# Attention of a fused three-layer kernel in units of four heads, its scores on all four tiles of TensorE's array

## The chip, the core and the metric

The kernel runs on one core of one Trainium2 chip. The metric is device time in microseconds, the median of several executions. The engines of the core are named as the profile names them: PE (TensorE, matrix products; PEld is its weight load), ACT (ScalarE), DVE (VectorE), POOL (GpSimd) and SP (SyncE, which issues the DMAs). PE writes to PSUM alone, eight banks of 2 KB per partition; ACT and DVE read it from there.

## What is computed

Three layers follow each other. The first is attention inside chunks of 64 tokens (8 sequences, 8 heads, 576 tokens, 64 features a head); the second a gated layer with a convolution over three tokens; the third a token and feature transform (real part of a two-dimensional FFT), a normalization and two products.

```python
q, k, v = (x.reshape(8, 8, 9, 64, 64) for x in (q, k, v))   # 9 chunks of 64 tokens
s = matmul(q, k.T) / 8
a = exp(s - max(s)); a = a / (sum(a) + 1e-9)
x = matmul(a, v)                                            # -> (8, 576, 512)
h = relu(x @ w_in)
x = (h * sigmoid(conv3(h, conv_w))) @ w_out
u = x + real(fft2(x))
un = (u - mean(u)) / sqrt(var(u) + 1e-6)
out = u + relu(un @ w_ch1) @ w_ch2
```

## The kernel before

A planner orders the work. Every piece is an `op` with an engine, an estimated cost, a priority and the buffers that it reads and writes; `Plan.emit` goes through them by earliest start and then by priority, and calls the function that issues the instructions. The order on each engine is thus fixed when the program is built; what a buffer's ring allows is part of it (a ring of n buffers lets the op for a new one start when the readers of the n-th before are through). PSUM has two rings of four banks: `x`, used in turn, and `o`, whose banks are taken in any order. For `o` an op may ask for `spare` banks beside those that it takes: it starts only when as many are free, which keeps banks for others.

**Attention** (`attention(i, hp, prio)`, L339) handles half a sequence `i` (four blocks of 64 tokens when `i` is even, five when it is odd; `n` is that number) and one pair of heads `hp`. q and k lie transposed with the features of the first head on partitions 0 to 63 and those of the second on 64 to 127. `qk_unit` (L350) makes the scores, one 64x64x64 fp32 matmul for each block and head; the rows of a head's features set the row half of the array, the output's partitions the column half, and both are the same half here. All go to one PSUM bank `s`. DVE takes the maximum (L360), ACT the exponential of each block with its row sum (L365), DVE normalizes (L368 to L370). `tr_unit` (L374) transposes two blocks at a time, ACT copies them out (L381, L383), and `pv_unit` (L389) multiplies with v. There the token block's parity sets the row half and the head the column half, and the outputs of the two row halves go to two banks (L385). ACT copies them (L400, L403), and from the second half sequence on DVE makes the low part of a high/low split (L404). PE sees an fp32 matmul as two records; a split fp32r product is one record each for high by high, high by low and low by high.

**The gated layer** is `m_step` (L409) and `x_step` (L472), eight feature tiles `f` for each half sequence, one after the other on PE; `m_step` accumulates in an `o` bank, `x_step` in four `x` banks. Attention of half sequence `i + 1` is queued among the steps of `i` (L919). In the first half sequence the weights are also brought from their 64-bit form to fp32 on DVE (`to_float32`, L263).

**The transforms** follow each whole sequence `b`: `fold` (L522), six `d_step`s (L541) over features and three `s_step`s (L568) over tokens, two `o` banks each, then `u_step` (L598), which transposes, adds and stores `u`.

**The last layer** multiplies by Strassen-like block sums with seven products. `prep` (L765) loads, normalizes and transposes a chunk `c` of tokens and makes sums of its four blocks; `left` (L687) splits each into high and low part. `group(c, g, t)` (L795) computes the seven products of one of eight weight groups; its `product` may carry an `after`: for the very first group, `last_d`, the last `d_step`. `second` (L844) multiplies with the second weights. The weight sums of groups 2 to 7 live in a pool `e` that takes the place of the transforms' pools, so their casts (`load_tw`, L673) come after the transforms' last store.

The lines of `pv_unit` that set its tiles, and the call that gates the first group:

```python
for h2, k in [(h2, k + par) for k in range(0, n, 2) for h2 in range(2) for par in range(min(2, n - k))]:
    j, par = divmod(k, 2)
    kk = slice(64 * par, 64 * par + 64)
    mm = slice(64 * h2, 64 * h2 + 64)
    pe.matmul(xp[par]()[mm, j, :], v()[kk, j, mm], at()[kk, j, mm], start=True, stop=True)
...
return op("PE", mm_cost(n, passes=6), unit, prio, r=[*w, *x], w=[acc], after=() if c or g else last_d)
```

Of the kernel before, what the change touches and what calls it, by code (L numbers as in the profile page):

```python
# [8 lines left out]
F32 = mybir.dt.float32  # L9
# [37 lines left out]
class Buf:  # L47
# [16 lines left out]
    def __call__(self):  # L64
# [4 lines left out]
        return self.tile  # L69

# [129 lines left out]
def kernel(  # L200
# [88 lines left out]
    def load_dft(prio):  # L289
# [18 lines left out]
        h = buf("d", "fg", 1, [128, 640], F32R)  # L308
# [10 lines left out]
    early += [("d", tag, 1) for tag in ("f00", "f10", "f01", "f11", "fg")]  # L319
# [16 lines left out]

    x0 = {}

    def attention(i, hp, prio):  # L339
        b, c = divmod(i, 2)  # L340
        n = NTOK[c] // 64
        m = 2 + c
        qk = buf(*(("s", "xlo", 2) if (i, hp) == (0, HP - 1) else ("a", "qk", 3)), [128, 2, NTOK[c]])
        load(qk, lambda: (qk_a, qk_b)[c][b, hp], 1024 * NTOK[c], prio - 12)
        v = buf("a", "v", 6, [128, m, 128])
        load(v, lambda: (v_a, v_b)[c][b, hp], 65536 * m, prio - 10)
# [12 lines left out]
        es, mx, sm = buf("a", "es", 4, [128, n, 64]), buf("a", "mx", 4, [128, n]), buf("a", "sm", 4, [128, n, 1])  # L359
        vop(64 * n, lambda: dve.tensor_reduce(out=mx(), in_=s(), op=ALU.max, axis=AX.X), prio, [s], [mx])  # L360
        vop(n, lambda: dve.tensor_scalar(mx(), mx(), -0.125, None, op0=ALU.mult), prio, [mx], [mx])

        def exp():
            for k in range(n):
                act.activation(out=es()[:, k, :], in_=s()[:, k, :], func=ACT.Exp, scale=0.125, bias=mx()[:, k:k + 1], accum_out=sm()[:, k, :])  # L365

        op("ACT", 291 * n, exp, prio, r=[s, mx], w=[es, sm])
        vop(n, lambda: dve.tensor_scalar(sm(), sm(), 1e-9, None, op0=ALU.add), prio, [sm], [sm])  # L368
# [5 lines left out]
        def tr_unit():  # L374
            flat = es().rearrange("p c k -> p (c k)")
            for j in range(m):
                w = 64 if j == 2 else 128
                pe.transpose(tp()[:w, j, :], flat[:, 128 * j:128 * j + w], ident)  # L378
# [712 lines left out]
```

## Time and profile before

| | |
|---|---|
| median of three runs | 1398.34 us (1395.86 to 1398.58) |
| the profiled execution, its own time | 1399.52 us |
| its span, first to last instruction | 1397.7 us |
| PE busy | 1364.1 us (98%) |
| DVE busy | 1058.5 us (76%) |
| ACT busy | 818.5 us (59%) |
| bytes moved by DMA | 207.86 MB |
| granted clock of TensorE, mean | 0.995 |

The span has four stretches. Up to about 56 us the first half sequence and the weight conversions; to 634 us the other half sequences with attention, gated layer and transforms; to 1037 us the end of the transforms and the first products of the last layer (L815); to the end its second products (L882). A busy time is the union of an engine's instructions; PE's records overlap, so the time that a burst takes from PE is read from the starts of the records around it. A wait in square brackets behind a row is idle time of that engine just before it, with what ended it.

### The profile page before, as it was taken

The page shows a single profiled execution, that of the slowest core. Times are in us where ns is not written, and L with a number is a line of the kernel's source. Part 1 is how long each engine was busy: PE and PEld are TensorE (multiplying, and loading weights), DVE is VectorE, ACT ScalarE, POOL GpSimd, SP SyncE. Part 2 cuts the span into 40 slices and gives each one's busy share as a digit, 9 for nine tenths or more (in the row PEclk, how much of TensorE's full clock was granted, in tenths as well). Part 3 has the DMA queues.
Part 4 walks back from the last instruction along what each step waited for, and adds up shares of the span by engine and source line. Part 5 has one row for each costly group of instructions (what it writes and reads, how often), then busy time and mean ns, then how long its engine had stood idle before and what let it go on. Part 6 is the DMA issues. An engine that isn't in the chain of part 4 may idle for free.

```text
span 1397.7 us, 30248 instructions
## 1 busy us (share of the span) xinstructions
PE 1364.1 (98%) x11488; PEld 1323.3 (95%) x11488; DVE 1058.5 (76%) x2174; ACT 818.5 (59%) x2278; POOL 60.8 (4%) x182
## 2 busy tenths in 40 slices
PE   6899999999999999998999999999999999999999
PEld 5799999999999999998899999999999999999998
DVE  7999887878977676767576767576589777777773
ACT  6878575767776676755675655655664333333331
POOL 0101010101101000100000000000000000000000
PEclk9999999999999999999999999999999999999999
DMA  8534424323432222115756656666965545544541
GB/s 304 165 96 128 144 82 135 112 96 112 143 105 67 67 68 87 43 57 204 224 178 203 188 178 184 184 206 221 300 201 187 169 137 162 166 156 141 170 139 38
DMA packets 154721, 207.86 MB, mean 149 GB/s; under 512 B 11600, under 2 KB 103376, under 8 KB 154576
## 3 DMA queue, kind: packets, MB, share of 16 engines
q1 hardware_dynamic: 154576, 205.93, 46.2%
q8 instruction: 91, 1.49, 0.4%
q14 instruction: 54, 0.44, 0.1%
HBM read 131.82 MB, written 74.06 MB: 147 GB/s over the span
## 4 chain that ended last, share of the span: by engine, by line
PE 89%; DVE 4%; ACT 3%; DMA 2%; issue 1%; POOL 0%; ACTq 0%; SPq 0%; DVEq 0%; POOLq 0%
PE x L815 20%; PE x L882 15%; PE x L492 14%; PE o L427 13%; PE o L882 11%; PE o L557 3%; PE o L586 3%; PE o L815 3%; PE o L356 2%; PE o L394 2%; PE o L606 1%; PE o L717 1%; PE o L378 1%; DVE raw L729 1%; DMA ts<-t_scr 1%; ACT es L365 1%
## 5 line engine op out<-in xcount | busy, mean ns | idle before, releaser
L255 ACT CAST sxh<-raw 128x1024 fp32r<-128x1024 f32 (+1 forms) x145 | 142.4, 994 | 190.1 <-PE o L882 81.9
L427 PE MATMUL o<-x,wih 128*128 128x320 f32 (+1 forms) x960 | 201.0, 302 | 1.7 <-ACT at L383 0.9
L815 PE MATMUL x<-sxh,th 128*128 128x384 f32 x576 | 195.2, 339 | 4.6 <-ACT th L255 2.1
L815 PE MATMUL x<-sxl,th 128*128 128x384 f32 x576 | 193.6, 336 | 1.6 <-DVE sxl L256 1.6
L815 PE MATMUL x<-sxh,tl 128*128 128x384 f32 x576 | 193.5, 336 | 0.3 <-DVE tl L256 0.3
L256 DVE TENSOR_TENSOR sxl<-raw,sxh 128x1024 fp32r<-128x1024 f32 (+1 forms) x145 | 165.6, 1153 | 30.2 <-ACT sxh L255 30.0
L882 PE MATMUL x<-th,sxl 128*128 128x256 f32 x576 | 163.1, 283 | 0.5 <-DVE sxl L256 0.5
L882 PE MATMUL x<-th,sxh 128*128 128x256 f32 x576 | 163.1, 283 | 0.0
L882 PE MATMUL x<-tl,sxh 128*128 128x256 f32 x576 | 163.0, 283 | 0.0
L791 DVE TENSOR_TENSOR u<-x,u 128x384 f32<-128x384 f32 (+1 forms) x168 | 83.6, 499 | 104.6 <-PE x L815 34.6
L427 PEld LDWEIGHTS o<-x,wih 128*128 128x128 f32 x960 | 152.8, 188 | 4.7 <-ACT at L383 1.2
L444 DVE SCALAR_TENSOR_TENSOR cv<-h,cw,cv 128x255 f32<-128x255 f32 (+2 forms) x256 | 130.8, 514 | 34.2 <-ACT cv L458 20.3
L492 PE MATMUL x<-gh,woh 128*128 128x322 f32 (+1 forms) x480 | 148.1, 309 | 0.1
L492 PE MATMUL x<-gl,woh 128*128 128x322 f32 (+1 forms) x480 | 142.3, 296 | 0.1
L492 PE MATMUL x<-gh,wol 128*128 128x322 f32 (+1 forms) x480 | 142.1, 296 | 0.0
L427 PE MATMUL o<-x,wil 128*128 128x320 f32 (+1 forms) x480 | 142.0, 296 | 0.0
L882 PE MATMUL o<-th,sxl 128*128 128x256 f32 x432 | 122.3, 283 | 0.0
L882 PE MATMUL o<-tl,sxh 128*128 128x256 f32 x432 | 122.2, 283 | 0.0
L882 PE MATMUL o<-th,sxh 128*128 128x256 f32 x432 | 122.2, 283 | 0.0
L815 PEld LDWEIGHTS x<-sxh,th 128*128 128x128 f32 x576 | 108.8, 189 | 7.0 <-ACT u L799 3.0
L815 PEld LDWEIGHTS x<-sxl,th 128*128 128x128 f32 x576 | 108.9, 189 | 2.4 <-DVE sxl L256 2.4
L882 PEld LDWEIGHTS x<-th,sxl 128*128 128x128 f32 x576 | 110.6, 192 | 0.7 <-DVE sxl L256 0.7
(266 smaller groups left out, 3301.5 us busy)
## 6 DMA issues: line engine op xcount, KB each, us to landing
raw<-h_scr SPq DMA_DIRECT2D x72, 512.0 KB, 4.4
h_scr<-u SPq DMA_DIRECT2D x96, 192.0 KB, 3.1
u<-u_scr SPq DMA_DIRECT2D x66, 256.0 KB, 4.6
qk<-in_qk_b SPq DMA_DIRECT2D x32, 320.0 KB, 3.0
h_scr<-m SPq DMA_DIRECT2D x48, 192.0 KB, 2.7
h_scr<-h SPq DMA_DIRECT2D x48, 192.0 KB, 2.9
out_y<-u SPq DMA_DIRECT2D x35, 256.0 KB, 2.4
wide<-in_w_ch SPq DMA_DIRECT2D x16, 512.0 KB, 5.1
```

The lines of the kernel that those rows point to most:

```text
L255: aop(n, lambda: act.copy(out=cut(h()), in_=cut(src())), prio, [src], [h], psum, after=after)
L256: vop(n, lambda: dve.tensor_tensor(cut(l()), cut(src()), cut(h()).bitcast(F32), op=ALU.subtract), prio, [src, h], [l])
L356: pe.matmul(s()[p, k, :], t[p, 0, ks], t[p, 1, ks], start=True, stop=True)
L394: pe.matmul(xp[par]()[mm, j, :], v()[kk, j, mm], at()[kk, j, mm], start=True, stop=True)
L427: pe.matmul(acc(), w[:, ws], x, start=k == 0, stop=k == 11)
L444: vop(hi - lo, lambda: dve.scalar_tensor_tensor(cv()[:, lo:hi], in0=h()[:, src:src + hi - lo], scalar=tap(k), in1=cv()[:, lo:hi], op0=ALU. ...
L492: pe.matmul(accs[d](), w[:, dsl], x, start=f == 0 and k == 0, stop=f == FT - 1 and k == 2)
L557: pe.matmul(acc()[:rows, :], x, w, start=n == 0, stop=n == len(todo) - 1)
L586: pe.matmul(accs[sine]()[:rows, :], w, x, start=n == 0, stop=n == len(todo) - 1)
L791: vop(n, lambda: dve.tensor_tensor(cut(x()), acc(), cut(x()), op=ALU.add), prio, [acc, x], [x])
L815: pe.matmul(acc(), a, b, start=first and m == 0, stop=m == 5, skip_group_check=not first)
L882: pe.matmul(acc(), a, b, start=first and m == 0 and gs[0] == 0, stop=gs[-1] == FG - 1 and m == len(todo) - 1, skip_group_check=not first)
```

## The change

Attention is called for `q` = 0 and 1, four heads each (two pairs `p`), instead of for four pairs. Scores: the two heads of each pair (`h`, the row half) go to two banks `s[0]` and `s[1]`, and blocks of even and odd number (`u`) to the two column halves, so four successive matmuls use the four 64x64 tiles; a fifth block is on column half `p`. Maximum, exponential and transposes go with it: the two maxima and exponentials are one operation per bank, scaling, reciprocal and normalization one per unit. v is laid out on the host so that `pv_unit` finds blocks 0 and 1 on one row half and 2 and 3 on the other; the zero padding of the fifth block goes (320 KB instead of 384 KB for two pairs). `spare` is 1 for scores and transposes, where it was 2. In `prep` the sums are S1 and S2 first, S3 in place of `a21`, and S4 in place of `a12` once that is split; the ring `ts` is no longer used there. Five of the first group's seven products come after the last `s_step`, B11 and B21 after the last `d_step` as before. The ring `fg` has two buffers instead of one.

```diff
-    def attention(i, hp, prio):
+    def attention(i, q, prio):
         b, c = divmod(i, 2)
         n = NTOK[c] // 64
...
-        s = buf("ps", "o" if i else "x", 4, [128, n, 64])
+        s = [buf("ps", "o" if i else "x", 4, [128, n, 64]) for _ in range(2)]
+        low, high = slice(0, 64), slice(64, 128)
+        half = (low, high)
         def qk_unit():
-            t = qk()
-            for k in range(n):
-                for h2 in range(2):
-                    p = slice(64 * h2, 64 * h2 + 64)
-                    ks = slice(64 * k, 64 * k + 64)
-                    pe.matmul(s()[p, k, :], t[p, 0, ks], t[p, 1, ks], start=True, stop=True)
-        op("PE", 160 * n, qk_unit, prio, r=[qk], w=[s], spare=2 if i else 0)
+            todo = [(h, p, 2 * j + u, 2 * p + j, u) for j in range(2) for p in range(2) for u in range(2) for h in range(2)]
+            if n == 5:
+                todo += [(h, p, 4, 4, p) for p in range(2) for h in range(2)]
+            for h, p, k, slot, u in todo:
+                t, ks = qk[p](), slice(64 * k, 64 * k + 64)
+                pe.matmul(s[h]()[half[u], slot, :], t[half[h], 0, ks], t[half[h], 1, ks], start=True, stop=True)
+        op("PE", 210 + 142 * n, qk_unit, prio, r=qk, w=s, spare=1 if i else 0)
...
+        for h in range(2):
+            vop(64 * n, lambda h=h: dve.tensor_reduce(out=mx()[:, h, :], in_=s[h](), op=ALU.max, axis=AX.X), prio, [s[h]], [mx])
+        vop(2 * n, lambda: dve.tensor_scalar(mx(), mx(), -0.125, None, op0=ALU.mult), prio, [mx], [mx])
+        for h in range(2):
+            def exp(h=h):
+                for k in range(n):
+                    act.activation(out=es()[:, at_es(h, k), :], in_=s[h]()[:, k, :], func=ACT.Exp, scale=0.125, bias=mx()[:, h, k:k + 1], accum_out=sm()[:, at_es(h, k), :])
+            op("ACT", 291 * n, exp, prio, r=[s[h], mx], w=[es, sm])
...
+        at = buf("a", "at", 2, [128, n, 128])
+        tps = [buf("ps", "o", 4, [128, 4, 128])] + ([buf("ps", "o", 4, [128, 1, 128])] if n == 5 else [])
         def tr_unit():
+            flat = es().rearrange("p a k -> p (a k)")
             for k in range(n):
+                pe.transpose(tps[k // 4]()[:, k % 4, :], flat[:, 128 * k:128 * k + 128], ident)
+        op("PE", 109 * n, tr_unit, prio + 2, r=[es], w=tps, spare=1)
+        aop(512, lambda: act.copy(out=at()[:, 0:4, :], in_=tps[0]()), prio + 2, [tps[0]], [at], True)
...
+        xp = [buf("ps", "o", 4, [128, 2, 2, 64]) for _ in range(2)] + ([buf("ps", "o", 4, [128, 2, 1, 64])] if n == 5 else [])
         def pv_unit():
+            for p in range(2):
+                for u in range(2):
+                    us = half[u]
+                    for h in range(2):
+                        for j in range(2):
+                            pe.matmul(xp[j]()[half[h], p, u, :], v[p]()[half[j], 128 * u + 64 * h:128 * u + 64 * h + 64], at()[half[j], 2 * h + p, us], start=True, stop=True)
+            if n == 5:
+                for p in range(2):
+                    for h in range(2):
+                        pe.matmul(xp[2]()[half[h], p, 0, :], v[p]()[half[h], 256:320], at()[half[h], 4, half[p]], start=True, stop=True)
+        op("PE", 210 + 142 * n, pv_unit, prio + 4, r=[*v, at], w=xp, after=[o for t in hl if t.before for o in t.before.readers])
...
-            g = buf(*(("s", "xlo", 2) if b == B - 1 and sine else ("d", "fg", 1)), [128, 2, 356])
+            g = buf("d", "fg", 2, [128, 2, 356])
...
-        s3, s2, s4 = buf("b", "ts", 3, [128, 2, HTOK]), raw(), raw()
+        s1, s2 = raw(), raw()
         n, p = 2 * HTOK, prios[-1]
-        tt(s3, a11, a21, ALU.subtract, n, p, [a11, a21], [s3])
-        tt(a21, a21, a22, ALU.add, n, p, [a21, a22], [a21])
-        tt(s2, a21, a11, ALU.subtract, n, p, [a21, a11], [s2])
-        tt(s4, a12, s2, ALU.subtract, n, p, [a12, s2], [s4])
-        for k, (i, x) in enumerate(((A11, a11), (A12, a12), (S2, s2), (S1, a21), (S3, s3), (A22, a22), (S4, s4))):
+        tt(s1, a21, a22, ALU.add, n, p, [a21, a22], [s1])
+        tt(s2, s1, a11, ALU.subtract, n, p, [s1, a11], [s2])
+        tt(a21, a11, a21, ALU.subtract, n, p, [a11, a21], [a21])
+        for k, (i, x) in enumerate(((A11, a11), (A12, a12), (S2, s2), (S1, s1), (S3, a21), (A22, a22))):
             left((c, i), x, n, p + k, [128, 2, HTOK])
+        tt(a12, a12, s2, ALU.subtract, n, p + 5, [a12, s2], [a12])
+        left((c, S4), a12, n, p + 6, [128, 2, HTOK])
...
-            return op("PE", mm_cost(n, passes=6), unit, prio, r=[*w, *x], w=[acc], after=() if c or g else last_d)
+            return op("PE", mm_cost(n, passes=6), unit, prio, r=[*w, *x], w=[acc], after=() if c or g else last_d if i in (B11, B21) else last_s)
...
-    for hp in range(HP):
-        attention(0, hp, -10 + 0.5 * hp)
+    for q in range(2):
+        attention(0, q, -10 + q)
...
-            for hp in range(HP):
-                attention(i + 1, hp, t + hp - 4)
+            for q in range(2):
+                attention(i + 1, q, t - 3.5 + 3 * q)
```

## Rows read from the trace of the kernel before

**Rows 1.** The page: busy time of PE, and the chain that ended last by engine.

```profile
PE 1364.1 (98%) x11488; PEld 1323.3 (95%) x11488; DVE 1058.5 (76%) x2174; ACT 818.5 (59%) x2278; POOL 60.8 (4%) x182
...
PE 89%; DVE 4%; ACT 3%; DMA 2%; issue 1%; POOL 0%; ACTq 0%; SPq 0%; DVEq 0%; POOLq 0%
```

**Rows 2.** By stretch: length, busy us of PE, PEld, DVE, ACT, POOL, granted clock, DMA.

```profile
0.00:56.00 56.00, 41.68 (x453) 32.58 (x454) 48.57 (x132) 40.82 (x157) 5.53 (x14) 1.00 0.72 250
56.00:634.00 578.00, 574.32 (x5768) 548.04 (x5768) 460.34 (x1210) 399.33 (x1477) 53.83 (x164) 1.00 0.30 97
```

**Rows 3.** Timeline of PE: start us, length us, engine, line, tiles, count.

```profile
119.34 0.28 PE L492 MATMUL x<-gh,wol 128*128 128x256 f32 x1
119.55 0.57 PE L394 MATMUL o<-at,v 64*64 64x64 f32 x20
...
120.27 0.28 PE L492 MATMUL x<-gl,woh 128*128 128x256 f32 x1
120.39 0.28 PE L492 MATMUL x<-gh,wol 128*128 128x256 f32 x1
...
121.46 0.28 PE L492 MATMUL x<-gh,wol 128*128 128x256 f32 x1
121.67 0.68 PE L356 MATMUL o<-qk 64*64 64x64 f32 x16
...
122.50 0.28 PE L492 MATMUL x<-gl,woh 128*128 128x256 f32 x1
```

**Rows 4.** Timeline of PE: longer and shorter bursts, and transposes.

```profile
80.62 0.46 PE L394 MATMUL o<-at,v 64*64 64x64 f32 x16
...
177.37 0.81 PE L378 MATMUL o<-ident,es 128*128 128x128 f32 x6
...
349.38 1.15 PE L356 MATMUL o<-qk 64*64 64x64 f32 x32
```

**Rows 5.** Groups of 56 to 634 us: line, operation, count | busy us, mean ns.

```profile
L394 PE MATMUL o<-at,v 64*64 64x64 f32 x1008 | 29.2, 228 | 0.0
...
L360 DVE TENSOR_REDUCE mx<-o 128x5 f32<-128x320 f32 x28 | 13.7, 489 | 6.2 <-PE o L356 5.9
...
L368 DVE TENSOR_SCALAR sm<-sm 128x5 f32<-128x5 f32 x28 | 4.8, 170 | 19.0 <-ACT es L365 18.8
```

**Rows 6.** The chain in order of time: start us, length us, what.

```profile
33.22 2.87 ACT es L365 x19
```

**Rows 7.** Timeline of PE, ACT and SP: end of the transforms.

```profile
649.98 1.85 PE L586 MATMUL o<-ab,ds 128*128 128x258 f32 x14
...
652.16 0.39 ACT L591 COPY q<-o 128x258 f32<-128x258 f32 x1
...
662.43 1.84 PE L586 MATMUL o<-ab,ds 128*64 128x258 f32 x14
...
669.58 0.48 SPq L619 DMA_DIRECT2D u_scr<-u  x1
...
671.85 1.03 ACT L255 CAST th<-ts 128x1024 fp32r<-128x1024 f32 x1
...
672.93 0.69 PE L815 MATMUL x<-sxh,th 128*128 128x384 f32 x1 [2.14 <-ACT th L255]
```

**Rows 8.** By stretch, columns as in rows 2: after the transforms.

```profile
671.00:678.00 7.00, 4.82 (x14) 4.32 (x15) 3.77 (x5) 3.62 (x5) 0.00 (x0) 0.64 0.72 224
```

**Rows 9.** Waits of PE, 634 to 1037 us: total, times, longest.

```profile
PE x L815 <- DVE sxl L256: 1.6, 3, 0.6
```

**Rows 10.** Timeline of DVE and PE at a change of token chunk.

```profile
847.51 0.95 DVE L729 TENSOR_TENSOR ts<-raw 128x768 f32<-128x768 f32 x1
848.49 2.94 DVE L729 TENSOR_TENSOR raw<-raw 128x768 f32<-128x768 f32 x3
...
851.36 0.44 PE L815 MATMUL x<-sxh,th 128*128 128x384 f32 x1 [0.20 <-ACT sxh L255]
852.36 0.44 PE L815 MATMUL x<-sxl,th 128*128 128x384 f32 x1 [0.55 <-DVE sxl L256]
```

More of the change, by code (lines that the diff above doesn't have):

```diff
@@ L69, in __call__, with __init__ @@
         return self.tile
+class Part:
+    def __init__(self, buf, p):
+        self.buf, self.p = buf, p
+    def __call__(self):
+        return self.buf()[:, self.p].rearrange("p c q -> p (c q)")
 class Op:
@@ new lines, in attention @@
+        aop(512, lambda: act.copy(out=at()[:, 0:4, :], in_=tps[0]()), prio + 2, [tps[0]], [at], True)
+        if n == 5:
+            aop(128, lambda: act.copy(out=at()[:, 4:5, :], in_=tps[1]()), prio + 2, [tps[1]], [at], True)
+        xp = [buf("ps", "o", 4, [128, 2, 2, 64]) for _ in range(2)] + ([buf("ps", "o", 4, [128, 2, 1, 64])] if n == 5 else [])
+        hl = [buf("a", f"x0{k}{c}{q}", 1, [128, 2, n, 64], F32R if i else F32) for k in range(2 if i else 1)]
+        for p, hp in enumerate(hps):
+            x0[i, hp] = [Part(t, p) for t in hl]
@@ L399, in attention @@
+        op("PE", 210 + 142 * n, pv_unit, prio + 4, r=[*v, at], w=xp, after=[o for t in hl if t.before for o in t.before.readers])
+        for j, x in enumerate(xp):
+            part = lambda t, j=j: t()[:, :, 2 * j:min(2 * j + 2, n), :]
+            k = 256 if j < 2 else 128
             if not i:
-                aop(k, lambda par=par: act.copy(out=hl[0]()[:, par::2, :], in_=xp[par]()), prio + 4, [xp[par]], [hl[0]], True)
+                aop(k, lambda x=x, part=part: act.copy(out=part(hl[0]), in_=x()), prio + 4, [x], [hl[0]], True)
@@ L401, in attention @@
                 continue
[L402 to L404 removed]
+            aop(k, lambda x=x, part=part: act.copy(out=part(hl[0]), in_=x()), prio + 4, [x], [hl[0]], True)
+            vop(k, lambda x=x, part=part: dve.tensor_tensor(part(hl[1]), x(), part(hl[0]).bitcast(F32), op=ALU.subtract), prio + 4, [x, hl[0]], [hl[1]])
@@ L430, in m_step @@
         if i:
-            done = op("PE", mm_cost(n, passes=12), m_unit, prio, r=[*wi[f], *(t for hp in range(HP) for t in x0[i, hp])], w=[acc], after=m_last)
+            done = op("PE", mm_cost(n, passes=12), m_unit, prio, r=[*wi[f], *(t.buf for hp in range(0, HP, 2) for t in x0[i, hp])], w=[acc], after=m_last)
             m_last[:] = [done]
@@ L993, in _host_layout @@
     vv = v.reshape(B, HP, 2, 9, 64, 64).transpose(0, 1, 3, 4, 2, 5).reshape(B, HP, 9, 64, 128)
-    pair = lambda x, n: x.reshape(B, HP, n, 128, 128).transpose(0, 1, 3, 2, 4)
-    v_b = np.zeros((B, HP, 128, 3, 128), v.dtype)
-    v_b[:, :, :, 0:2] = pair(vv[:, :, 4:8], 2)
-    v_b[:, :, :64, 2] = vv[:, :, 8]
+    four = lambda x: x.reshape(B, HP, 2, 2, 64, 128).transpose(0, 1, 2, 4, 3, 5).reshape(B, HP, 128, 256)
+    fifth = vv[:, :, 8].reshape(B, HP, 64, 2, 64).transpose(0, 1, 3, 2, 4).reshape(B, HP, 128, 64)
     feat = _feature_order()
@@ L1004, in _host_layout @@
         "qk_b": c(qk[..., 256:]),
-        "v_a": c(pair(vv[:, :, 0:4], 2)),
-        "v_b": v_b,
+        "v_a": c(four(vv[:, :, 0:4])),
+        "v_b": c(np.concatenate([four(vv[:, :, 4:8]), fifth], axis=-1)),
         "w_in": bits(cols(w_in)),
```

68 lines of the change are left out of this document (22 added, 46 removed).

## The prediction

> **What bounds the kernel now.** Read the page's first part first: TensorE (PE) is busy for 1364.1 of 1397.7 us, and the chain that ended last runs over PE for 89% of its length [rows 1]. Then the same by stage, since an average hides stages with other limits [rows 2]. In the first 56 us VectorE (DVE) is the busiest engine (48.6 us) and PE has gaps. From 56 to 634 us, where fourteen of the sixteen half sequences pass through attention, `m_step` and `x_step`, PE is busy for 574.3 of 578 us, DVE for 460 and ScalarE (ACT) for 399: PE has 4 us to give away, the others over 100. So in that stretch an instruction taken off PE shortens the run, and one taken off DVE or ACT does not. The reader should also see that PE's busy figure there is only a sign that it is fed; what a burst costs must be read from start to start of its neighbours.
>
> **What an attention burst costs PE today.** Rows 3 show two bursts between `x_step` matmuls (L492) that follow each other every 0.12 us. From the L492 at 121.46 to the one at 122.50 are 1.04 us; two of those slots are L492's own, so the scores of one head pair with four blocks (L356, 16 records, two for each fp32 matmul) cost 0.80 us. The product with v for five blocks (L394, 20 records) costs 0.93 - 0.24 = 0.69 us in the same way. Another size: 16 v records are busy 0.46 us against 0.57 for 20, so four blocks cost 0.58 [rows 3, 4]. Six transposes span 0.81 us, some 0.11 each [rows 4].
>
> Now the rate inside a burst. 32 score records span 1.15 us and 16 span 0.68: 0.029 us each. The 16 v records span 0.46 us; without the length of the last one (mean 0.228, [rows 5]) that is 0.23 over 15 steps, 0.0155 each, half as much. The shapes are the same, 64x64. The difference is the tile: `qk_unit` has rows and columns of the same half (two of the four 64x64 tiles), `pv_unit` alternates the row half and then the column half, all four. So two records share a step of 0.058 us in the one and four in the other. 16 records of scores are 8 steps, 0.47 us; the other 0.33 of 0.80 is entering and leaving the burst, paid by each burst that stands alone. The scores of five blocks, two steps more, cost 0.92.
>
> **Part 1, units of four heads.** The new `qk_unit` runs through (row half, column half) in the order that `pv_unit` has now, with one PSUM bank for each row half as there. So I take v's rate. Four blocks and four heads: 32 records in 8 steps, 0.80 us, the price of half as many heads today; five blocks: 40 records in 10 steps, 0.92. `pv_unit` gains no rate: 0.58 + 4 x 0.058 = 0.81 for four blocks; for five 0.69 + 6 x 0.058 = 1.04 (its fifth block uses the diagonal tiles only, so 12 steps in all). Transposes: four or five a unit, 0.44 or 0.55, where two pairs had four or six.
> Before: pairs at 0.80 + 0.22 + 0.58 = 1.60 and 0.92 + 0.33 + 0.69 = 1.94; 28 of each after the first two half sequences: 44.8 + 54.3 = 99.1 us. After: units at 2.05 and 2.51, 14 of each: 28.7 + 35.1 = 63.8. The difference is 35.3, of which 14.7 is the faster scores and the rest fewer entries and transposes. Some attention bursts already stand back to back and share an entry (the 32 records of [rows 4]; about nine such places by the timeline); I take 2.7 us off for those that the larger units can't repeat: **-32.6 us**. No switch cost is added: the same two kinds of shapes alternate, half as often.
> DVE and ACT do less as well: per half sequence three operations on 4 or 5 elements go from four to two, and copies merge. A DVE instruction on 5 elements takes 0.17 us [rows 5]; 154 fewer instructions in the 578 us are 25 of its 460 us. That stays under cover of PE and is worth nothing there.
> What it adds: a unit takes two of the four `o` banks for its scores, up to two for the transposes and three for v (before: one, one, two), and `exp` keeps ACT twice as long. An exponential with its sum takes 0.30 us (19 records in 2.87, [rows 6]), and a maximum over five blocks 0.49 [rows 5], so a five-block unit holds its banks for 0.7 + 2 x 0.49 + 0.2 + 10 x 0.30, about 5 us, and the evacuations of `m_step` queue on ACT behind them. Meanwhile PE has an `x_step` (own `x` banks) and two `m_step`s for the two banks left, each of 12 matmuls of 0.12 us or more. This just covers it, and attention is queued some nine steps ahead of its use. Bounds: 0, and 15 us if every second of the 28 units costs PE a microsecond. I take **+4**, nearer to 0 because two pairs' exponentials already run back to back in the 2.87 us row.
>
> **Part 2, the start.** DVE sets the pace there. It loses six small operations and two to four merged ones for each of the first two half sequences, 18 x 0.17, about 3 us; against that the first exponential waits for two loads and two maxima, where one of each did. **-2**, bounds -3.5 and +2. The second `fg` buffer, and the smaller v loads, hide behind that.
>
> **Part 3, the first product group behind `s_step`.** Today the first and the last of the three `s_step`s of the last sequence start at 649.98 and 662.43, with products of group 0 between them [rows 7]. The last u store is issued at 669.58, and only after it do the buffers of pool `e` exist: ACT casts the third weight group at 671.85, PE waits 2.14 us for it and then runs at the lower clock: 0.64 granted in 671 to 678, that is some 5 of 7 us at 1.2 GHz, 2.5 us lost [rows 7, 8]. With five of the seven products of group 0 (and all later ones) queued behind the last `s_step`, that one comes some 5 us earlier by my estimate (three bursts of 1.85 us and the copies between them, from 650 us on), the store and the cast too, and the wait of 2.14 and the slow stretch, together 5 us, should go. What is late next: between the `s_step`s PE has only transposes, while the banks of the one before are emptied; I put about 2 us of idle time there, from copies of 0.39 us [rows 7], one on ACT and two on DVE each time. **-3**, bounds -5.5 and, if the gaps between the `s_step`s are as long as the products that fill them now and the clock falls in them, +8.
>
> **Part 4, block sums in place.** At a change of token chunk DVE makes four sums (0.95, then 2.94 for three) before it can split S2; PE waits 0.20 + 0.55 us [rows 10]. The new order has S2 after two sums, 0.97 us sooner, so the wait goes at the three places where it stands (1.6 us for the larger part, [rows 9]). S4's sum moves behind the split of A12, whose cast is done before this stretch; DVE has no queue there that PE waits for. **-2**, bounds -2.3 and 0.
>
> **Sum.** -32.6 + 4 - 2 - 3 - 2 = -35.6 from the profiled execution's 1399.5 us: 1363.9. That execution is 1.2 us above the median of the runs, so **1363 us**.
>
> **Rivals.**
> *The four tiles don't run four at a time.* If the new scores keep today's 0.029 us a record, a unit costs 0.47 or 0.58 us more, 14 of each 14.7 us: 1378. Against it stands the v burst with its 0.0155 in the same order of tiles. The Trainium skill, "TensorE: Matmul & The Clock Gate", section "Wait — 56ns, not 53.3ns?", says that start-to-start never drops below about 25 ns however small the matmul; by that floor the scores would gain almost nothing (the sum would be about 1373). The v rows at 15.5 ns contradict it here, four tiles together. 5%.
> *Emptying PSUM becomes the bound.* The mechanism is in part 1: with two `o` banks held by scores for 5 us and ACT busy with exponentials, `m_step`'s accumulators wait. Without the +4, the change gains 39.6 us over 28 units, so from 1.4 us of PE idle time per unit on it loses; at 1.6 it gives 1399.5 - 39.6 + 45 = 1405, slower. For it: ACT's exponentials per unit are longer than PE's scores. Against: ACT has 179 us idle in the stretch and DVE 118, and both get less to do. The Trainium skill, "TensorEngine Tiling (Array Packing)", section "PSUM Bottleneck", warns of just this after a speedup by tiles. The trace so far bears it out little: PE lacks 4 us in 578. 5%; a milder form at about 1 us per unit, 1385 to 1398, 6%.
> *The gating of group 0 costs more than it gives.* At its upper bound of +8 the sum is 1374. 12%.
> *Every part at its lower bound,* no new idle time anywhere: 1353, mostly below the range. 4%.
> The forecast, 1354 to 1373, has the remaining 68%.
>
> **How the numbers follow.** The lower bounds together, -32.6 - 3.5 - 5.5 - 2.3 = -43.9, give 1354, and 1352 if the larger units share as many entries as the pairs. The upper ones, -32.6 + 15 + 2 + 8, give 1391, but hardly all at once. I set the range to 1353 to 1386, which leaves out the slower case, part of the milder one and the extremes. A measurement of this kernel tells about 0.2%, 2.8 us, from no change. Faster by more: 0.91 (forecast, first and third rival, most of the milder second, the last). Within: 0.04. Slower: 0.05.
>
> **What would show it.** Right: L356 bursts of 32 and 40 records of about 0.68 and 0.80 us busy; half as many bursts of L356, L378 and L394; PE still over 98% busy from 56 us to the last `x_step`, and that end some 34 us earlier; no wait on the third weight cast. Wrong: L356 bursts of 1.1 us and more (first rival); PE waits on ACT h, ACT es or ACT at of many times 1 us (second); gaps between the L586 bursts with a fallen clock (third). The forecast fails altogether if the entry cost of a burst grows with its length, which the 32-record burst speaks against.

## The result, and the profile after

The changed kernel takes 1363.43 us (1362.99 to 1365.32), the kernel before 1398.46 in the same series: a ratio of 0.9754, 95% interval 0.9738 to 0.9771. The profiled execution took 1363.09 us, its span is 1361.3.

The page of after, answering to [rows 1]: PE is still the engine that ends last, with 39 us less to do.

```profile
PE 1325.3 (97%) x11472; PEld 1298.0 (95%) x11472; DVE 1037.4 (76%) x2002; ACT 805.7 (59%) x2182; POOL 70.8 (5%) x182
...
PE 91%; DVE 5%; ACT 2%; issue 1%; DMA 0%; POOL 0%; ACTq 0%; DVEq 0%
```

By stretch (columns as in [rows 2]; the last `x_step`, now L518, ends at 607):

```profile
56.00:607.00 551.00, 544.96 (x5769) 528.12 (x5768) 440.93 (x1055) 386.65 (x1390) 60.13 (x163) 1.00 0.32 101
```

PE is 6.0 us short of the stretch, where it lacked 3.7 of 578 before: a little of the gain came back as idle time. Where the rest of it lies is read from four starts and ends of PE's records, in both traces:

| us of the span | before | after | stretch that ends there |
|---|---|---|---|
| first split `m_step` (L427, now L453) starts | 61.92 | 58.47 | start, -3.45 |
| last `x_step` (L492, now L518) ends | 634.75 | 606.97 | middle, -24.33 |
| first product with the second weights (L882, now L908) starts | 1027.50 | 991.01 | third stretch, -8.71 |
| last matmul ends | 1394.42 | 1357.97 | second products, 0.0 |

The bursts themselves, in the timeline of PE of after (columns as in [rows 3]; L373 scores, L416 and L420 the product with v, its fifth block last):

```profile
94.86 0.28 PE L453 MATMUL o<-x,wil 128*128 128x256 f32 x1
95.07 0.81 PE L373 MATMUL o<-qk 64*64 64x64 f32 x40
95.81 0.51 PE L453 MATMUL o<-x,wih 128*128 128x256 f32 x2
96.16 0.28 PE L453 MATMUL o<-x,wil 128*128 128x256 f32 x1
...
102.15 0.31 PE L518 MATMUL x<-gh,wol 128*128 128x322 f32 x1
102.39 0.69 PE L416 MATMUL o<-at,v 64*64 64x64 f32 x32
102.90 0.41 PE L420 MATMUL o<-at,v 64*64 64x64 f32 x8
103.25 0.51 PE L453 MATMUL o<-x,wih 128*128 128x256 f32 x2
103.59 0.28 PE L453 MATMUL o<-x,wil 128*128 128x256 f32 x1
```

From 94.86 to 96.16 are 1.30 us; three slots of 0.12 belong to L453, so 40 score records cost 0.94. From 102.15 to 103.59, less one slot of 0.15 and two of 0.12, 1.05 for v. Over all lone bursts the medians are 0.82 and 0.94 for scores, 0.44 and 0.55 for transposes, 0.82 and 1.05 for v; all bursts after the first split `m_step` sum to 62.5 us where they took 93.4, PE's idle time left out.

Between the starts and ends of the table, PE is idle for 6.01 us of the middle, before for 1.92. The largest of the waits is a single one of 2.26 us in the last `x_step` of the first half sequence (L512), for DVE's conversion of a weight; the expectations below call it the first `x_step`'s. Before and after, the last step of that conversion on DVE and the `x_step` that reads it:

```profile
66.35 0.68 DVE L272 SCALAR_TENSOR_TENSOR fw<-wx,fw 128x512 f32<-128x512 f32 x1
69.91 1.89 PE L486 MATMUL x<-gh,fw 128*128 128x256 f32 x8
...
65.29 0.68 DVE L282 SCALAR_TENSOR_TENSOR fw<-wx,fw 128x512 f32<-128x512 f32 x1
66.03 1.99 PE L512 MATMUL x<-gh,fw 128*128 128x256 f32 x8 [2.26 <-DVE fw L282]
```

DVE is through with it only 1.06 us sooner than before, PE came 3.45 us sooner to its first split `m_step`: so this wait gives back 2.3 us of what the start had gained. The others (line that waited, releaser: total, times, longest) stand for the most part where scores meet the transforms; the largest groups:

```profile
PE o L453 <- DVE u L637: 1.5, 3, 0.7
PE o L632 <- DVE u L637: 0.8, 1, 0.8
PE o L632 <- ACT es L385: 0.7, 2, 0.4
```

Behind the last `x_step`, in the third stretch, PE waits 5.22 us for ACT before the last transform, before and after alike. The end of the transforms, against [rows 7] (PE, SP's queue; L612 is `s_step`, L632 the transposes of `u_step`):

```profile
622.52 3.73 PE L612 MATMUL o<-ab,ds 128*128 128x258 f32 x28
627.33 0.66 PE L632 MATMUL o<-ident,xlo 128*128 128x128 f32 x4 [1.08 <-ACT t L620]
...
628.93 0.44 PE L841 MATMUL o<-sxh,th 128*128 128x384 f32 x1 [0.51 <-DVE u L637]
...
632.72 1.06 PE L612 MATMUL o<-ab,ds 128*64 128x258 f32 x7 [0.77 <-DVE u L637]
...
638.12 0.49 SPq L645 DMA_DIRECT2D u_scr<-u  x1
```

Two `s_step`s now follow each other, PE idles 1.08 + 0.51 + 0.77 us between the last ones, and nothing waits for the third weight cast. Counted from the last `x_step`, the store goes out at 31.15 us, before at 34.83.

### The profile page after: what moved, and what is told of

Read it like the earlier page. It is cut to its first block, busy times and chain, and to the rows that moved or that the text cites. A ratio compares the mean times of both kernels' runs of the same rounds, so it can differ in the third digit from the quotient of the medians.

```text
span 1361.3 us, 29843 instructions
## 1 busy us (share of the span) xinstructions
PE 1325.3 (97%) x11472; PEld 1298.0 (95%) x11472; DVE 1037.4 (76%) x2002; ACT 805.7 (59%) x2182; POOL 70.8 (5%) x182
## 4 chain that ended last, share of the span: by engine, by line
PE 91%; DVE 5%; ACT 2%; issue 1%; DMA 0%; POOL 0%; ACTq 0%; DVEq 0%
PE x L841 21%; PE x L908 15%; PE x L518 14%; PE o L453 14%; PE o L908 11%; PE o L841 4%; PE o L583 3%; PE o L612 3%; PE o L416 1%; PE o L373 1%; PE o L743 1%; PE o L632 1%; PE o L398 1%; ACT es L385 1%; DVE cv L470 0%
## 5 line engine op out<-in xcount | busy, mean ns | idle before, releaser
L265 ACT CAST sxh<-raw 128x1024 fp32r<-128x1024 f32 (+1 forms) x150 | 147.4, 989 | 186.5 <-PE o L908 83.2
L453 PE MATMUL o<-x,wih 128*128 128x320 f32 (+1 forms) x960 | 198.4, 300 | 1.9 <-DVE u L637 1.5
L266 DVE TENSOR_TENSOR sxl<-raw,sxh 128x1024 fp32r<-128x1024 f32 (+1 forms) x150 | 170.9, 1146 | 36.8 <-ACT sxh L265 36.8
L908 PE MATMUL x<-th,sxl 128*128 128x256 f32 x576 | 163.1, 283 | 0.5 <-DVE sxl L266 0.5
L908 PE MATMUL x<-th,sxh 128*128 128x256 f32 x576 | 163.1, 283 | 0.1
L908 PE MATMUL x<-tl,sxh 128*128 128x256 f32 x576 | 163.0, 283 | 0.0
L453 PEld LDWEIGHTS o<-x,wih 128*128 128x128 f32 x960 | 153.0, 188 | 4.5 <-DVE u L637 2.2
L518 PE MATMUL x<-gh,woh 128*128 128x322 f32 (+1 forms) x480 | 145.3, 303 | 0.0
L518 PE MATMUL x<-gh,wol 128*128 128x322 f32 (+1 forms) x480 | 142.2, 296 | 0.0
L518 PE MATMUL x<-gl,woh 128*128 128x322 f32 (+1 forms) x480 | 142.2, 296 | 0.0
L453 PE MATMUL o<-x,wil 128*128 128x320 f32 (+1 forms) x480 | 142.0, 296 | 0.0
L908 PE MATMUL o<-th,sxl 128*128 128x256 f32 x432 | 122.3, 283 | 0.0
L908 PE MATMUL o<-tl,sxh 128*128 128x256 f32 x432 | 122.3, 283 | 0.0
L908 PE MATMUL o<-th,sxh 128*128 128x256 f32 x432 | 122.2, 283 | 0.0
L908 PEld LDWEIGHTS x<-th,sxl 128*128 128x128 f32 x576 | 110.6, 192 | 0.7 <-DVE sxl L266 0.7
L908 PEld LDWEIGHTS x<-th,sxh 128*128 128x128 f32 x576 | 110.6, 192 | 0.5 <-ACT h L826 0.5
L908 PEld LDWEIGHTS x<-tl,sxh 128*128 128x128 f32 x576 | 110.6, 192 | 0.0
```

The lines of the kernel that those rows point to most:

```text
L265: aop(n, lambda: act.copy(out=cut(h()), in_=cut(src())), prio, [src], [h], psum, after=after)
L266: vop(n, lambda: dve.tensor_tensor(cut(l()), cut(src()), cut(h()).bitcast(F32), op=ALU.subtract), prio, [src, h], [l])
L453: pe.matmul(acc(), w[:, ws], x, start=k == 0, stop=k == 11)
L518: pe.matmul(accs[d](), w[:, dsl], x, start=f == 0 and k == 0, stop=f == FT - 1 and k == 2)
L908: pe.matmul(acc(), a, b, start=first and m == 0 and gs[0] == 0, stop=gs[-1] == FG - 1 and m == len(todo) - 1, skip_group_check=not first)
```

## The experiments

The stretches of the profiled executions, measured as in the table above. The second products take 366.9 us in each.

| kernel | start | middle | third stretch | median of the runs |
|---|---|---|---|---|
| before | 61.92 | 572.83 | 392.75 | 1398.46 |
| after | 58.47 | 548.50 | 384.04 | 1363.43 |
| e11_again (after) | 58.55 | 548.56 | 383.76 | 1363.31 |
| e1_order | 60.07 | 555.36 | 384.08 | 1372.33 |
| e2_sums | 59.46 | 550.14 | 387.96 | 1369.58 |
| e3_gate | 59.41 | 550.17 | 386.04 | 1367.64 |
| e4_attention | 58.65 | 554.49 | 389.89 | 1375.18 |
| e5_entry | 59.95 | 558.81 | 383.90 | 1374.61 |
| e6_one_exp | 58.15 | 539.31 | 384.03 | 1353.66 |
| e7_fg | 59.38 | 555.57 | 384.05 | 1368.55 |
| e8_gate3 | 61.62 | 548.50 | 384.03 | 1365.44 |
| e9_sub | 64.92 | 544.14 | 384.00 | 1365.13 |
| e10_old_fg2 | 62.68 | 574.45 | 388.90 | 1397.89 |
| e12_sub3 | 58.89 | 544.94 | 383.80 | 1360.65 |

In the profiles of e1, e2, e3, e5, e7, e8 and e9 the granted clock is 0.86 from 28 to 40 us (1.00 in the others), which with what follows costs 1 to 3 us in the start and the first `x_step`s; single parts are therefore compared by stretch. e11_again, the changed kernel once more:

> The changed kernel once more, for comparison with the others of this series: 1363 to 1365.5 us.

### Is it four at a time, and what does a burst cost?

```diff
-            todo = [... for j in range(2) for p in range(2) for u in range(2) for h in range(2)]
+            todo = [... for u in range(2) for j in range(2) for p in range(2) for h in range(2)]
```

> The changed kernel with the same score matmuls in another order: the column half changes slowest, so that successive matmuls use the two row halves of one column half only. Same instructions, same banks, same order on every other engine. My theory (four tiles at a time is what makes scores cheap): the first 32 records of each unit take 16 steps of 0.058 us instead of 8, 0.47 us more for each of the 28 units after the start, so about 13 us slower than the changed kernel, 1376, and score bursts of 32 records busy 1.15 instead of 0.68 us. Rival (the order in which tiles come doesn't matter, or a floor per record sets the pace): no difference, or for a floor of about 25 ns 32 records in 0.8 us plus the entry, already slower than seen.

1372.33 us (1371.50 to 1373.19), ratio 0.9821 (0.9804 to 0.9837), 8.9 us above the changed kernel; 6.9 of it in the middle. Its timeline of PE:

```profile
96.75 0.28 PE L453 MATMUL o<-x,wil 128*128 128x256 f32 x1
96.96 1.09 PE L373 MATMUL o<-qk 64*64 64x64 f32 x40
97.98 0.51 PE L453 MATMUL o<-x,wih 128*128 128x256 f32 x2
98.32 0.28 PE L453 MATMUL o<-x,wil 128*128 128x256 f32 x1
```

The same 40 records cost 1.57 - 0.36 = 1.21 us, 0.27 more than in the order of the change, and 32 cost 1.10 instead of 0.82. So the order over the tiles carries this part. The price is smaller than expected, and the single records tell why. Starts in the burst at 83.17 us, where the records of the first column half stand ahead of all those of the second in the program:

```
83.168 .175 | .275 .281 | .333 .340 | .391 .398 | .450 .456 .462 .469 | .508 .515 | .566 .569 .573 .575 | .625 .627 .631 .634 | .685 ...
```

Two records each 0.058 us, as in the scores before; but from 83.462 on four run beside each other, after 10 of the 16 records of the first half. By my reading the pair at .462 and .469 is the second half's first (like the very first pair it is 0.267 us long, the others up to .685 are 0.218), begun while the first half's tiles still have records to come. The burst then needs fewer steps than two to a step would give. That records can start ahead of others that precede them in the program is plain where two bursts adjoin, since they have different lines. In the program all 32 score records (L373) stand ahead of the first record of v (L416); in the trace of e1 six of them start behind it:

```profile
62.10 0.80 PE L373 MATMUL o<-qk 64*64 64x64 f32 x26
62.69 0.27 PE L416 MATMUL o<-at,v 64*64 64x64 f32 x1
62.74 0.22 PE L373 MATMUL o<-qk 64*64 64x64 f32 x2
```

In the changed kernel the 32 records at 128.39 start four within 0.02 us, every 0.058 us.

Entering and leaving: a transpose that nobody reads cuts each burst in two.

```diff
+            for m, (h, p, k, slot, u) in enumerate(todo):
+                if i and m == 8:
+                    pe.transpose(s[0]()[:, 6:8, :]..., ident, ident)
```

> Every score burst from the second half sequence on is cut in two by one 128x128 fp32 transpose (0.11 us), whose result nothing reads. The prediction prices a unit as its steps plus 0.33 us for entering and leaving the burst. If that price is paid by every burst that stands alone, each of the 28 units after the first gated-layer step gets 0.33 + 0.11 = 0.44 us longer, some 12.4 us in all, and the time is about 1376 us. Rival: the 0.33 us belongs to what surrounds the burst in today's order (the buffers, the first record's long latency) and not to the switch itself; then the cut costs its transpose alone, 28 x 0.11 = 3.1 us, about 1366.5 us.

1374.61 us (1373.96 to 1375.09), ratio 0.9832 (0.9819 to 0.9846). The slots of the scores in the middle go from 18.4 to 29.7 us, 0.42 for each of 27 bursts:

```profile
96.79 0.28 PE L455 MATMUL o<-x,wil 128*128 128x256 f32 x1
97.00 0.46 PE L375 MATMUL o<-qk 64*64 64x64 f32 x16
97.39 0.33 PE L373 MATMUL o<-ident 128*128 128x128 f32 x1
97.65 0.58 PE L375 MATMUL o<-qk 64*64 64x64 f32 x24
98.16 0.50 PE L455 MATMUL o<-x,wih 128*128 128x256 f32 x2
98.50 0.28 PE L455 MATMUL o<-x,wil 128*128 128x256 f32 x1
```

The transpose with its neighbours takes what a lone one does (0.11) and 0.31 more. The entry price is real, and a burst of 64x64 tiles pays it again where a 128x128 transpose interrupts it; the rival falls.

### The parts one by one

```diff
-            ... after=() if c or g else last_d if i in (B11, B21) else last_s)
+            ... after=() if c or g else last_d)
```

> The changed kernel with all products of the first group behind the last feature transform again, not behind the last token transform. My theory: the token transforms start as late as before, the last store and with it the third weight cast too, PE waits 2.1 us and runs at the lower clock for some us: 3.5 us slower, 1367. Rival (gating loses as much as it gives, since PE idles between the token transforms): no difference, 1363 within 1.5 us. Second rival: another cause moved the store, then PE shows no wait on the third cast.

1367.64 us (1367.52 to 1369.56), ratio 0.9788 (0.9774 to 0.9803). In the third stretch, where the edit is, it is 2.00 us longer. The wait for the cast is back, and the lower clock behind it: a line of its waits of PE, one of its stretches, and the stretch of after at the same distance from the last `x_step`:

```profile
PE x L841 <- ACT th L265: 2.1, 1, 2.1
```

```profile
643.00:652.00 9.00, 6.07 (x24) 5.24 (x25) 4.93 (x6) 5.03 (x8) 0.00 (x0) 0.81 0.48 135
```

```profile
640.00:649.00 9.00, 9.00 (x53) 8.96 (x53) 6.41 (x8) 7.83 (x15) 0.00 (x0) 1.00 0.83 264
```

```diff
-        s1, s2 = raw(), raw()
+        s3, s2, s4 = buf("b", "ts", 3, [128, 2, HTOK]), raw(), raw()
...
```

> The changed kernel with the block sums as they were (S3 in a ts buffer, four sums ahead of the splits), nothing else undone. Theory A (my step 4, priced from start to start): the three chunk changes cost 1.3 us each again, 3.9 us. Theory B (the ts ring matters too): the two waits of PE on ACT's evacuations near the end of the first products (0.67 and 0.60 us in brackets before, gone after) come back too, 1.9 us, together 5.8. If neither, the gain at the chunk changes came from somewhere else and the time stays at 1363.

1369.58 us (1367.37 to 1369.98), ratio 0.9796 (0.9781 to 0.981). The third stretch is 3.92 us longer. At each of the three changes of chunk PE shows the pair of waits of [rows 10]:

```profile
821.84 0.34 PE L840 MATMUL o<-sxh,tl 128*128 128x384 f32 x1
822.38 0.44 PE L840 MATMUL x<-sxh,th 128*128 128x384 f32 x1 [0.20 <-ACT sxh L265]
823.38 0.44 PE L840 MATMUL x<-sxl,th 128*128 128x384 f32 x1 [0.55 <-DVE sxl L266]
823.66 0.34 PE L840 MATMUL x<-sxh,tl 128*128 128x384 f32 x1
```

From 821.84 to 823.66 are 1.82 us for three slots of 0.17, so one change costs 1.30 though the brackets say 0.75: each wait also costs the 0.27 by which a matmul that starts alone is longer than its slot. Three times 1.30 is 3.9, but that it equals the 3.92 is chance. One of the two waits for ACT's evacuations that the second theory named is back as well (0.60 us in brackets at 974.54). Set record against record of after, a change of chunk costs 1.19 and this wait 0.77, together 4.3; where the other 0.4 comes back was not followed up. So the first theory carries most, and a part of the second holds.

Attention alone, with the old gate, sums and single `fg` buffer:

> The attention part of the change alone: block sums, gating and the fg ring as before. If the parts add up: 1363.4 + 3.9 to 5.8 (sums) + 3.5 (gate) = 1371 to 1373, that is 26 to 28 us faster than the kernel before; the last x_step ends at about 607 us of the span as in the changed kernel. Rival (the parts overlap or the fg ring matters): the last x_step ends later than 607, or the sum misses by over 2 us.

1375.18 us (1374.66 to 1379.18), ratio 0.9845 (0.9827 to 0.9863), outside the expectation. The third stretch has 5.85 more than after, which is e2's 3.92 and e3's 2.00. But the middle, where neither acts, is 6.0 longer, and PE's idle time there 11.0 instead of 6.0 us; behind the longest of the added waits (1.76 us, at 357.8) the granted clock is 0.72 from 358 to 364 us, which loses another 1.7 us, and 0.7 is won elsewhere. Only the ring `fg` was left:

```diff
-            g = buf("d", "fg", 2, [128, 2, 356])
+            g = buf(*(("s", "xlo", 2) if b == B - 1 and sine else ("d", "fg", 1)), [128, 2, 356])
```

> The ring fg has one buffer as before, all else as in the changed kernel. The prediction gave the second buffer nothing, since it lies behind other work: then 1363.4 us, within 1.5 us. Theory from the run with the attention change alone, whose middle was 6.2 us longer than the changed kernel's although its start took the same time: the single buffer makes the second fold wait for the six-matmul groups of the first, which puts the transforms in another order on TensorE; then the middle is about 6 us longer and the time is about 1369.5 us.

1368.55 us (1367.31 to 1371.09), ratio 0.9792 (0.9778 to 0.9805); the middle is 7.1 us longer, 1.6 of it in the first `x_step`s, which belong to its start. So the second buffer, to which I gave nothing, is worth 5.5 to 6 us. Is that a gain of its own? The same edit the other way round, in the kernel before:

> The kernel before with a second fg buffer alone (v has five buffers in place of six to make room; nothing waits for a v load). With one buffer in the changed kernel the middle is 6 to 7 us longer. If that is a gain of its own, the kernel before gets it too, some 4 to 6 us: 1392 to 1394 us. Rival: the trace of before shows no wait for it (TensorE lacks 1.9 us in its whole middle), the second buffer only repairs what the units of four bring; then there is no change, 1397 to 1399.5 us.

1397.89 us (1396.13 to 1400.22), ratio 0.9999 (0.999 to 1.0008). In the kernel before it is worth nothing (the middle is 1.6 longer, not shorter): it repairs what the units of four bring. The timeline of e7 at one of its longer waits, PE, then DVE, then ACT:

```profile
207.71 0.70 PE L373 MATMUL o<-qk 64*64 64x64 f32 x32
208.34 0.66 PE L632 MATMUL o<-ident,xlo 128*128 128x128 f32 x4
208.83 0.60 PE L632 MATMUL o<-ident,xhi 128*128 128x128 f32 x4
211.02 0.56 PE L453 MATMUL o<-x,wih 128*128 128x320 f32 x2 [1.59 <-DVE u L637]
```

```profile
208.46 0.42 DVE L379 TENSOR_REDUCE mx<-o 128x4 f32<-128x256 f32 x1 [1.23 <-PE o L373]
209.42 0.42 DVE L379 TENSOR_REDUCE mx<-o 128x4 f32<-128x256 f32 x1
210.29 0.68 DVE L637 TENSOR_TENSOR u<-t,o 128x512 f32<-128x512 f32 x1
...
210.71 0.30 ACT L385 ACTIVATE es<-o,mx 128x64 f32<-128x64 f32 x1
```

Scores have taken two `o` banks and `u_step` the other two; the next `m_step` finds none. The addition of u that frees one comes behind the two maxima on DVE, and the score banks stay held, since the exponentials begin at 210.71. This is read from one place of the trace. With the second buffer the transforms stand in another order on PE, and the seven waits around u's transposes that after still has are 0.27 to 0.84 us each.

### Who holds the banks

```diff
-            vop(64 * n, lambda h=h: dve.tensor_reduce(out=mx()[:, h, :], in_=s[h](), op=ALU.max, axis=AX.X), prio, [s[h]], [mx])
...
-                for k in range(n):
-                    act.activation(..., in_=s[h]()[:, k, :], func=ACT.Exp, scale=0.125, bias=mx()[:, h, k:k + 1], accum_out=...)
+                act.activation(out=es()[:, 4 * h:4 * h + 4, :], in_=s[h]()[:, 0:4, :], func=ACT.Exp, scale=0.125)
...
+        vop(128 * n, lambda: dve.tensor_reduce(out=sm()..., in_=es(), op=ALU.add, axis=AX.X), prio, [es], [sm])
```

> Leaves out the maximum and its subtraction: one exponential per bank (and one for a fifth block) straight from the scores, the row sums by one DVE reduction; 61 ACT instructions in the place of 488 after the start, the score banks free earlier by about 1 us for each unit. If ACT's exponentials and the two score banks that they hold cause the 4 us of new idle time in the middle (the prediction's +4), TensorE's idle time between the first and the last step of the gated layer falls from 6.0 to about 2 us and the time to about 1359 us or less. Rival: that idle time comes from DVE (the additions of u and the first weight conversion, which the waits name) and the exponentials are under cover: no change in the middle beyond 1 us; only the start, where DVE and ACT set the pace, gains 1 to 2 us, so 1361.5 to 1363 us.

1353.66 us (1353.39 to 1354.06), ratio 0.9683 (0.967 to 0.9696). Of the 6.0 us of PE's idle time in the middle nothing is left; u's transposes and `m_step` wait for nothing, although DVE's additions of u, after which the waits were named, are all there. The 2.3 of the weight wait is gone too; DVE has no maxima to take here, so for that one this run doesn't tell the engines apart. Of the middle's 9.2 us, 6.0 are this idle time; most of the rest is scores that moved ahead of the first `m_step` (1.3) and `u_step` (1.1). To do the same with the whole computation, DVE subtracts the maximum from the bank:

```diff
+            if i >= 2:
+                vop(64 * n, lambda h=h: dve.tensor_tensor(s[h](), s[h](), <mx of h, broadcast>, op=ALU.subtract), prio, [s[h], mx], [s[h]])
```

> Computes everything: from the third half sequence on DVE subtracts the maximum from the score bank in place (one operation per bank), ACT then needs one exponential per bank and one for a fifth block, and DVE sums the rows (one reduction per unit). About 110 us of ACT's work in the middle go, DVE gets some 42 us more (its middle would be about 480 of 545 us busy). Theory: the idle time of TensorE in the middle (6.0 us before the last transform) is ACT's, through the exponentials and the banks that they hold, although the waits name DVE's additions; then it falls under 2 us, and the time is 1356 to 1360 us. Rival: the waits name the right engine, DVE, and it gets more to do here; then the idle time stays or grows, 1363 to 1368 us.

1365.13 us (1361.42 to 1365.74), ratio 0.9753 (0.9735 to 0.9772). The time lies in the rival's range; the idle time in the middle, 3.4 us, is neither under 2 nor as it was. The middle is 4.4 us shorter, but the start 6.4 longer, in another order on PE from its first gated-layer steps on and with the granted clock at 0.79 from 48 to 64 us. So the edit again, from the fourth half sequence on (`i >= 3`):

> As e9_sub, but with the subtraction on DVE from the fourth half sequence on, so that the start (first three half sequences) issues the same work in the same order as the changed kernel; there the start had grown by 6.4 us and hid what the middle gained. The 2.3 us wait of the first x_step stays, since it lies before that. Theory: the other idle time of TensorE in the middle (3.8 us, waits named after DVE's additions of u) is ACT's exponentials and the banks that they hold; it falls under 1.5 us and the time is 1359 to 1361.5 us. Rival: it is DVE's own work; it stays or grows, 1363 us or more.

1360.65 us (1359.69 to 1362.30), ratio 0.974 (0.9726 to 0.9753). This version computes everything; it is 2.8 us faster than the changed kernel by the medians, a small difference, but its slowest run (1362.30) lies below the quickest of after and e11_again (1362.97). Its waits in the middle, and its stretch up to the last `x_step`:

```profile
PE x L523 <- DVE fw L282: 2.3, 1, 2.3
PE x L529 <- DVE gl L266: 0.6, 1, 0.6
PE o L464 <- ACT q L628: 0.5, 1, 0.5
PE x L529 <- ACT gh L265: 0.3, 1, 0.3
```

```profile
56.00:604.00 548.00, 544.21 (x5771) 529.05 (x5770) 470.54 (x1110) 341.87 (x1000) 58.25 (x163) 1.00 0.31 101
```

The idle time apart from the weight wait falls from 3.8 to 1.3 us, with DVE 30 us busier than in the same stretch of after, and ACT 45 us less (not 110: that figure had added up records that overlap). So ACT's exponentials caused it, and not the load of DVE, whose additions the waits named. By which way is open: the score banks are held for a shorter time, ACT has less to do, and with the new costs the planner also puts the work on PE in another order from 91 us on. These were not tried apart. Nor were the smaller `spare` and the new priorities of attention, which change with the units, undone by themselves.

### The idle time between the last `s_step`s

```diff
-            ... last_d if i in (B11, B21) else last_s)
+            ... last_d if i in (B11, B21, T2) else last_s)
```

> Three products of group 0 come after the last d_step (T2 also), four after the last s_step, where the change has two and five. TensorE is idle 1.08, 0.51 and 0.77 us between the last s_steps now; a product takes 1.05 us. If those gaps are only a lack of something to do, T2 fills the first of them and the first second-product burst comes 1.0 to 2.0 us earlier: about 1362 us. Rival: T2 delays the middle s_step and with it the last one, and the third weight cast is late again, as where all seven products were free: the gain is lost, 1363 to 1365.5 us.

1365.44 us (1364.14 to 1366.21), ratio 0.9766 (0.9753 to 0.978). T2 does fill the first gap (1.08 to 0.23 us), but a wait of 0.57 for ACT's copy of u in group 0 and one of 0.19 before a transpose take its place: the third stretch is 384.03 against 384.04. The gain is lost, as the rival said, but not in its way: nothing waits for the third cast, and the store goes out 30.64 us behind the last `x_step`, 0.5 sooner than in after. Filling the gap gains nothing, since something just behind is late instead.

## Why the prediction held, and where only its sum did

| term | predicted | measured | from |
|---|---|---|---|
| attention bursts in the middle | -32.6 | -30.9 | burst sums, 93.4 to 62.5 |
| new idle time where scores meet the transforms | +4 | +1.8; with one `fg` buffer +6.5 to +6.9 | idle time of the middle less the weight wait of 2.3: after; e7, e4 |
| the rest of the middle (`u_step` +1.7, switches) | 0 | +2.5 | middle -24.33 less the other terms |
| start, with the weight wait that follows | -2 | -1.2 (-3.45 and +2.3) | after; attention alone -3.3 and +2.3, e4 |
| first group | -3 | -2.0 | e3 |
| block sums | -2 | -3.9 | e2 |
| not foreseen, third stretch | 0 | -2.9 | before less e4 |
| sum of the terms | -35.6 | -36.6 (span to last matmul -36.5) | |

*The bursts.* All six unit prices came out within 0.02 us, because they were read from start to start of the neighbours, and the rate of the new scores was that of a burst with the same shapes and tile order. The first rival (no four at a time) is out: e1, with pairs, costs 8.9 us. The floor of 25 ns that the Trainium skill gives ("TensorE: Matmul & The Clock Gate", "Wait — 56ns, not 53.3ns?") does not hold across four tiles: 32 records start over 0.48 us here, 15 ns each.

*The +4.* PE's idle time in the middle did grow by 4.1 us, but that is luck: 2.3 of it is the wait for a weight conversion, which belongs to part 2, and only 1.8 is what the term was for. Its reasoning was not right either. I looked for waits of `m_step` on ACT, and took the cover of an `x_step` and two `m_step`s for enough. What ran short of banks was the place where scores meet the transforms, which take two `o` banks as well; there was no such wait in before, and I had not gone through the `o` users one by one. Without the second `fg` buffer the term would have been 6.5 to 6.9. "Hide behind that" for this buffer is the step that failed: it looked only at the start, and a zero read from the trace of before (true there, e10) was taken to hold for a kernel whose bank demand had doubled. The second rival is thus the right mechanism, as far as e7's timeline and e12 show it, at about a quarter of a microsecond per unit, 6.5 to 6.9 over 28, not 1. It also bounds the rule that an instruction taken off ACT or DVE is worth nothing there: that held for a kernel with 1.9 us of idle time, and no longer in after, where e6's middle is 9.2 and e12's 3.6 us shorter.

*The end of the middle.* "That end some 34 us earlier" was wrong: 27.8. The sum itself had only -32.6 + 4 - 2 = -30.6 there, so this line contradicted its own terms; the remaining 2.8 are the +2.5 of the rest, 1.7 on the bursts and 0.8 at the start, less 2.2 on the idle time.

*The start* was sized by the number of DVE instructions, and that DVE sets the pace is borne out: its last weight conversion ends 1.06 us sooner, which is close to the -1.2 that remain of PE's 3.45. e4 shows that attention gives it all.

*The first group.* The mechanism was as told: wait and slow clock gone, 2.4 us of new gaps. The term was too large by 1 since the store comes 3.7 us earlier and not 5, and since part of what it removes isn't always there. In e3, where it was measured, the lower clock makes up 1.7 of the 2.0 (0.81 granted in 9 us), so where the clock doesn't fall the gate is worth some 0.3 by this estimate. In e10, which has the same program and the same order on PE as before in this stretch, the same wait of 2.14 us is followed by no fall. Twenty microseconds of before and of e10 (columns as in [rows 2]):

```profile
664.00:684.00 20.00, 17.04 (x81) 15.83 (x80) 8.39 (x12) 9.86 (x18) 0.00 (x0) 0.83 0.57 180
...
664.00:684.00 20.00, 16.66 (x99) 15.59 (x98) 10.21 (x16) 11.30 (x22) 0.00 (x0) 1.00 0.70 216
```

At 0.83 the lower of the two clock levels (1.2 GHz) takes up a third of the 20 us, so 3.4 us are lost where the prediction, from the 7 us of [rows 8], took 2.5; in e4 the clock is 0.91 from 645 to 665 us. The unforeseen 2.9 lies for the most part here: e10's third stretch, without the change, is 3.85 us shorter than in the profiled execution of before, which also has a wait of 0.67 us for ACT near the end that e4 and e10 lack. So most of it is no gain of the change; whether the units of four give any of it stays open.

*The block sums* were priced by the bracketed idle time, 0.75, where start to start gives 1.30; the same care as for the bursts would have found it. The wait for ACT that goes with them (0.8) was not in the term.

So the time of 1363 came out with errors of both signs: start and middle together 2.8 us short of the forecast (27.8 against 30.6), made up by the block sums and by a third stretch that was long in the one execution of before from which the sum was counted. That the total fits within a microsecond is luck; that the bursts carry most of it is not.

## What to carry to other kernels

Price a burst, and a wait too, from start to start of the neighbours; the bracketed idle time leaves out the matmul that restarts alone. When a unit takes twice the PSUM banks, list every user of that ring and look where the largest two meet; the wait will bear the name of whoever frees a bank last, not of whoever holds the others. A spare buffer that the trace shows idle can become worth microseconds once another part of the same change shifts the pressure.

## What the runs showed of the hardware

Matmul records on different 64x64 tiles can start ahead of the program's order: in e1 a record of v starts at 62.69 us, and six score records that stand before it in the program start from 62.74 on. By the same reading the second column half of a burst begins after 10 of the first half's 16 records, which is why two by two cost 0.28 us a burst and not 0.47. Across four tiles records start 15 ns apart on average (32 in 0.48 us), on two tiles 29 ns ([rows 3, 4]). Cutting a burst of 64x64 matmuls by one 128x128 transpose costs 0.42 us, nearly four times the transpose alone. And the clock need not fall after a wait of PE: after the same 2.14 us it was granted 0.83 in before and 1.00 in e10, each over 664 to 684 us.
